# Sliding-window attention and highway FFN: one sequence of loads, half-wide stages at both ends, x transposed by DMA in the second half

## Chip, core and metric

The kernel runs on one core of a Trainium2 chip. The metric is device time in microseconds (us), the median of three runs. The engines are TensorE (PE, with its weight loads as PEld), VectorE (DVE), ScalarE (ACT), GpSimd (POOL) and SyncE (SP). POOL issues the loads that change the type from float32 to bf16, SP issues the stores; 16 DMA engines move both.

## The reference

```python
# q, k, v: (batch 8, heads 8, seq 576, head_dim 64), float32
scores = scale * np.matmul(q, k.transpose(0, 1, 3, 2))
rel = pos[:, None] - pos[None, :]
slopes = 2.0 ** (-8.0 * (np.arange(H) + 1) / H)
bias = slopes[:, None, None] * (-np.abs(rel))[None, :, :]
mask = (rel >= 0) & (rel < 128)
attn = softmax(np.where(mask, scores + bias[None], -1e9))
x = np.matmul(attn, v).transpose(0, 2, 1, 3).reshape(4608, 512)
H = np.maximum(x @ w_h, 0.0)
T = 1.0 / (1.0 + np.exp(-(x @ w_t + b_t)))
out = T * H + (1.0 - T) * x          # (4608, 512) float32
```

## The kernel before

Two batches form a duo, and there are four duos (m = 0 to 3). In a duo the rows of the tiles hold the head dimension of both batches, 64 rows each. A sequence of 576 is cut into four blocks of 128 and a tail of 64. A duo has two stages: s = 0 computes the query blocks 0 and 1 of both batches, s = 1 the blocks 2 and 3 and both tails as one block of 128 rows. A unit is one head in one stage: scores (`scores`, L274), the exponential on ACT into `pt` (`soft`, L284), the mask times decay on DVE (`mask`, L295), P.V on PE (`pv`, L310, with a column of ones that gives the sum), and the division on DVE (`norm`, L335 and L336) into `x`. That is 64 units.

q and k come in by POOL's DMAs as `ql` and `kl` (`load_qk`, L75 whole, L83 in parts of heads), their last 64 rows as `qtl` and `ktl` (`load_tails`, L95), v as `va` in five pieces (`load_v`, L104). PE transposes them (L210, L219) and DVE or ACT copies the result out (`evac`). Two sets of these tiles serve the duos in turn.

When the eight heads of a stage are normalised, its four or five blocks of 128 rows go through the FFN, 36 blocks in all: four transposes of `x` on PE (L346) and a copy on ACT (L356) give `xt`; four matmuls with wH give `pa` (L364); DVE makes max(pa, 0) - x in `uu` (L372); four matmuls with wT and one with the bias row, which contracts over a single row (L383), give `pz` (L381); ACT takes the tanh into `tt` (L390); POOL turns it into a sigmoid (L394); DVE multiplies `uu` by it (L399); POOL adds x into `ot` (L403); SP stores it (L413, L419).

The order on every engine comes from a planner at the end of the function: each piece has an engine, a cost in ns, a priority in time slots, and pieces that it needs; a list is simulated and the pieces are written out by simulated start. PSUM tiles lie in separate rings: one double bank for scores, two banks for transposes, two for P.V, one each for `pa` and `pz`. In the instruction stream each engine works strictly in its order, so a piece that waits holds all that stand behind it.

Of the kernel before, what the change touches and what calls it, by code (L numbers as in the profile page):

```python
# [10 lines left out]
P = 128  # L11
# [3 lines left out]
def kernel(  # L15
# [25 lines left out]
    SLOT, LOOK = 2200, 100  # L41
    NBLK = (4, 5)
    slopes = [float(2.0 ** (-8.0 * (h + 1) / H)) for h in range(H)]

    cp = ctx.enter_context(tc.tile_pool(name="const", bufs=1))
    p0p = ctx.enter_context(tc.tile_pool(name="p0", bufs=12))
    p1p = ctx.enter_context(tc.tile_pool(name="p1", bufs=5))
    smp = ctx.enter_context(tc.tile_pool(name="small", bufs=4))
    xp = ctx.enter_context(tc.tile_pool(name="x", bufs=3))
    fx = ctx.enter_context(tc.tile_pool(name="fx", bufs=3))  # L50
    op = ctx.enter_context(tc.tile_pool(name="ot", bufs=4))
    ft = ctx.enter_context(tc.tile_pool(name="ft", bufs=3))
    RING = {"sc": 1, "tr": 2, "av": 2, "a": 1, "z": 1}
    ps_sc, ps_tr, ps_av, ps_a, ps_z = (
        ctx.enter_context(tc.tile_pool(name="ps_" + n, bufs=b, space=PSUM))
        for n, b in RING.items()
    )
    RING.update({"p0": 12, "p1": 5, "x": 3, "xt": 3, "uu": 3, "tt": 3, "ot": 4})

# [10 lines left out]
    def load_qk(m, hs=slice(0, H), which=(0, 1)):  # L70
        i = m % 2
        for w in which:
            src, dst = ((q, QL), (k, KL))[w]
            if hs == slice(0, H):
                nc.gpsimd.dma_start(  # L75
                    out=dst[i][:].rearrange("p r h n -> p (r h) n"),
                    in_=src[2 * m : 2 * m + 2, :, 0:512, :].rearrange(
                        "r h (p t) d -> p (r h) (t d)", t=4
                    ),
                )  # L80
                continue
            for r in range(2):
                nc.gpsimd.dma_start(  # L83
                    out=dst[i][:, r, hs, :],
                    in_=src[2 * m + r, hs, 0:512, :].rearrange(
                        "h (p t) d -> p h (t d)", t=4
                    ),
                )

    def load_tails(m, which=(0, 1)):  # L90
        i = m % 2
        for w in which:
            src, dst = ((q, QTL), (k, KTL))[w]
# [16 lines left out]


# [82 lines left out]
    TR = {}  # L194
    EV = {
        (m, w, hp): "ACT" if w and (m or hp == 0) else "DVE"
        for m in range(ND) for w in (0, 1) for hp in range(5)
    }

    def transposes(m, w, hp):  # L200

        i = m % 2
        pt = ps_tr.tile([P, 1024], BF16, name="pt")
        TR[m, w, hp] = pt
        if hp < 4:
            L = (QL, KL)[w][i]
            for hl in range(2):
                for t in range(4):
                    for r in range(2):
                        nc.tensor.transpose(  # L210
                            out=pt[r * D : (r + 1) * D,
                                   hl * 512 + t * P : hl * 512 + (t + 1) * P],
                            in_=L[:, r, 2 * hp + hl, t * D : (t + 1) * D],
                            identity=ident[:],
                        )
        else:
# [8 lines left out]
    def evac(m, w, hp):  # L225
        i = m % 2
        pt = TR.pop((m, w, hp))
        cp_ = nc.scalar.copy if EV[m, w, hp] == "ACT" else nc.vector.tensor_copy
        if hp < 4:
            if w == 0:  # L230
                nc.vector.tensor_copy(
                    out=QT[i][:, 2 * hp : 2 * hp + 2, 0:512],
                    in_=pt[:].rearrange("p (h n) -> p h n", h=2),
                )
            else:
                cp_(
                    out=KT[i][:, 2 * hp : 2 * hp + 2, 0:512].rearrange(
                        "p h (c t) -> p h c t", t=4
                    ),
                    in_=pt[:].rearrange("p (h t c) -> p h c t", h=2, t=4),  # L240
                )
# [7 lines left out]
    def unit(u):
        m, r = divmod(u, 2 * H)  # L250
        s, h = divmod(r, H)
        return m, s, h

    SC, PT = {}, {}

    def scores(u):
        m, s, h = unit(u)
        i = m % 2
        sc = ps_sc.tile([P, 2, 512], F32, name="sc")
        SC[u] = sc  # L260
        qm = QT[i][:, h, 0:512].rearrange("p (t c q) -> p c t q", t=4, c=4)

        if s == 0:
            mm = ((0, 0, 2, 0), (1, 1, 2, 256))
        else:
            mm = ((2, 2, 2, 0), (3, 3, 1, 256), (3, None, 0, 384), (4, None, 0, 448))
        for j, c, n, off in mm:
# [12 lines left out]
    def soft(u):  # L280
        m, s, h = unit(u)
        pt = (p0p, p1p)[s].tile([P, 2, 512], BF16, name=f"pt{s}")
        PT[u] = pt
        nc.scalar.activation(  # L284
            out=pt[:], in_=SC.pop(u)[:], func=ACTF.Exp,
            bias=BIAS[:, h : h + 1], scale=scale,
        )

    def mask(u):
        m, s, h = unit(u)  # L290
        pt = PT[u]
        n = 2 - s
        o = pt[:].rearrange("p r (j w) -> p (r j) w", j=n)
        mk = MK[:, h : h + 1, 0 : 512 // n].to_broadcast([P, 2 * n, 512 // n])
        nc.vector.tensor_tensor(out=o, in0=o, in1=mk, op=ALU.mult)  # L295

    AV, X = {}, {}

    def pv(u):
        m, s, h = unit(u)  # L300
        i = m % 2
        va = VA[i]
        av = ps_av.tile([P, 5, D + 1], F32, name="av")
        AV[u] = av
        me = PT[u]

        def group(g, r, terms, rows=slice(0, P)):
            for n, (pt, off, j) in enumerate(terms):
                w = rows.stop - rows.start
                nc.tensor.matmul(  # L310
                    out=av[rows, g, :], lhsT=pt[:, r, off : off + w],
                    rhs=va[:, j, r, h, :],
                    start=n == 0, stop=n == len(terms) - 1,
                )

        for r in range(2):
            if s == 0:
                group(2 * r, r, ((me, 0, 0),))
                group(2 * r + 1, r, ((me, 128, 0), (me, 256, 1)))
            else:  # L320
                group(2 * r, r, ((PT[u - H], 384, 1), (me, 0, 2)))
                group(2 * r + 1, r, ((me, 128, 2), (me, 256, 3)))
        if s == 1:
            for r in range(2):
                group(4, r, ((me, 384, 3), (me, 448, 4)), slice(r * D, (r + 1) * D))
# [282 lines left out]
```

## Time and profile before

| | us |
|---|---|
| median of three runs (212.16 to 212.93) | 212.35 |
| the profiled execution, whole | 213.98 |
| its span in the trace | 212.3 |

| engine | busy us | share of the span | instructions |
|---|---|---|---|
| PE | 173.5 | 82% | 2004 |
| DVE | 142.4 | 67% | 308 |
| ACT | 124.2 | 58% | 161 |
| POOL | 119.5 | 56% | 137 |

The busy times are sums over the span. PE's is inflated where its clock is low, and matmuls are pipelined, so the time from the start of one group to the start of the next says more than the length of one. In the timeline, what stands in brackets behind a row is the time for which the engine waited before it, and what ended the wait. The SP queue issues 136 stores and nothing else.

### The profile page before, as it was taken

To read this page: it belongs to the slowest core of one execution; us is meant where nothing else is said; L and a number is where in the kernel's file an instruction comes from. 1 tells how busy PE (TensorE), PEld (TensorE's weight loads), DVE (VectorE), ACT (ScalarE), POOL (GpSimd) and SP (SyncE) were. 2 spreads that over 40 slices of the span, in tenths; PEclk is the share of its full clock that TensorE was granted. 3 is DMA by queue.
4 is the path that set the end of the run, shared out by engine and by line. 5 is a ranking of instruction groups with operands and counts; after the bars stand their busy time and mean duration, and the time that the engine had idled before them with its cause. 6 is when DMAs were issued, how large, how long until landed. Compare 5 with 4: busy or idle time off the path is not lost.

```text
span 212.3 us, 5013 instructions
## 1 busy us (share of the span) xinstructions
PE 173.5 (82%) x2004; PEld 95.4 (45%) x2004; DVE 142.4 (67%) x308; ACT 124.2 (58%) x161; POOL 119.5 (56%) x137
## 2 busy tenths in 40 slices
PE   0547765995079679999999999999999999997940
PEld 0325443573045422556565445566453455543410
DVE  5626767570094164898886988897789979873550
ACT  2340355657023544889878868877878778824420
POOL 7993493429365395845333896543345564554662
PEclk9999999999555855999999999999999999999995
DMA  5599999999999999994223999322223333324244
GB/s 60 57 195 175 181 173 141 199 172 136 121 196 212 212 165 167 127 199 124 63 54 73 109 114 186 82 54 49 57 70 77 73 79 73 79 51 99 52 98 99
DMA packets 70135, 24.97 MB, mean 118 GB/s; under 512 B 48096, under 2 KB 65504, under 8 KB 70112
## 3 DMA queue, kind: packets, MB, share of 16 engines
q0 software_dynamic: 63328, 15.21, 90.9%
q1 hardware_dynamic: 6784, 9.45, 18.1%
q8 instruction: 15, 0.25, 0.5%
q14 instruction: 8, 0.07, 0.1%
HBM read 30.41 MB, written 9.44 MB: 188 GB/s over the span
## 4 chain that ended last, share of the span: by engine, by line
PE 57%; DMA 25%; POOL 10%; issue 2%; ACT 2%; DVE 1%; POOLq 1%; SPq 0%; ACTq 0%; DVEq 0%
DMA kl<-in_k_dram 19%; PE pz L381 14%; PE pa L364 13%; PE sc L274 8%; PE av L310 8%; DMA va<-in_v_dram 6%; PE pz L383 5%; PE pt L210 4%; PE pt L346 4%; POOL va L104 3%; POOL ql L83 2%; POOL kl L83 1%; POOL ot L403 1%; ACT pt L284 1%; POOL tri L142 1%
## 5 line engine op out<-in xcount | busy, mean ns | idle before, releaser
L284 ACT ACTIVATE pt<-sc,bias 128x1024 bf16<-128x1024 f32 x64 | 71.3, 1115 | 40.9 <-PE sc L274 40.7
L403 POOL TENSOR_TENSOR ot<-uu,x 128x512 f32<-128x512 bf16 x36 | 45.4, 1262 | 21.6 <-DVE uu L399 18.1
L295 DVE TENSOR_TENSOR pt<-pt,mk 128x1024 bf16<-128x1024 bf16 x64 | 49.1, 769 | 6.0 <-ACT pt L284 5.5
L394 POOL TENSOR_SCALAR tt<-tt 128x512 f16<-128x512 f16 x36 | 23.1, 641 | 37.6 <-ACT tt L390 34.7
L310 PE MATMUL av<-va,pt 128*128 128x65 bf16 (+1 forms) x576 | 33.2, 206 | 9.5 <-DVE pt L295 8.0
L364 PE MATMUL pa<-wH,xt 128*128 128x512 bf16 x144 | 39.6, 400 | 1.2 <-ACT xt L356 0.7
L381 PE MATMUL pz<-wT,xt 128*128 128x512 bf16 x144 | 39.8, 401 | 0.2 <-ACT tt L390 0.2
L310 PEld LDWEIGHTS <-pt 128*128 128x128 bf16 (+1 forms) x576 | 25.5, 105 | 23.4 <-DVE pt L295 8.9
L390 ACT ACTIVATE tt<-pz 128x512 f16<-128x512 f32 x36 | 21.6, 599 | 22.0 <-PE pz L383 20.4
L372 DVE SCALAR_TENSOR_TENSOR uu<-pa,x 128x512 bf16<-128x512 f32 x36 | 24.7, 686 | 14.1 <-PE pa L364 14.0
L274 PE MATMUL sc<-qt,kt 64*128 64x256 bf16 (+2 forms) x384 | 28.5, 258 | 5.1 <-ACT pt L284 3.4
L336 DVE TENSOR_TENSOR x<-av,rd 128x256 bf16<-128x256 f32 (+1 forms) x64 | 29.3, 458 | 2.2
L104 POOL DMA_DIRECT2D va<-in_v_dram x20 | 22.2, 1112 | 12.7 <-DMA kl<-in_k_dram 4.2
L399 DVE TENSOR_TENSOR uu<-uu,tt 128x512 bf16<-128x512 bf16 x36 | 16.1, 448 | 17.6 <-POOL tt L394 16.8
L356 ACT COPY xt<-pt 128x512 bf16<-128x512 bf16 x36 | 20.9, 583 | 6.3 <-PE pt L346 6.2
L335 DVE RECIPROCAL rd<-av 128x4 f32<-128x4 f32 (+1 forms) x64 | 11.7, 183 | 15.6 <-PE av L310 15.1
L274 PEld LDWEIGHTS <-kt 64*128 64x128 bf16 x384 | 13.7, 98 | 16.2 <-issue 11.5
L381 PEld LDWEIGHTS <-xt 128*128 128x128 bf16 x144 | 12.3, 101 | 14.4 <-issue 4.3
L346 PE MATMUL pt<-ident,x 128*128 128x128 bf16 x144 | 15.3, 231 | 3.7 <-DVE x L336 3.7
L364 PEld LDWEIGHTS <-xt 128*128 128x128 bf16 x144 | 12.3, 100 | 12.8 <-issue 3.6
L210 PE MATMUL pt<-ident,ql 128*64 128x128 bf16 x256 | 11.8, 244 | 6.9 <-POOL ident L127 5.0
L210 PE MATMUL pt<-ident,kl 128*64 128x128 bf16 x256 | 12.9, 256 | 3.9 <-DMA kl<-in_k_dram 2.2
(42 smaller groups left out, 123.1 us busy)
## 6 DMA issues: line engine op xcount, KB each, us to landing
out_dram<-ot SPq DMA_DIRECT2D x128, 64.0 KB, 1.7
va<-in_v_dram POOLq DMA_DIRECT2D x16, 256.0 KB, 9.3
ql<-in_q_dram POOLq DMA_DIRECT2D x3, 1024.0 KB, 15.6
kl<-in_k_dram POOLq DMA_DIRECT2D x3, 1024.0 KB, 18.1
out_dram<-ot SPq DMA_DIRECT2D x8, 128.0 KB, 2.3
ql<-in_q_dram POOLq DMA_DIRECT2D x2, 384.0 KB, 5.6
kl<-in_k_dram POOLq DMA_DIRECT2D x2, 384.0 KB, 7.9
qtl<-in_q_dram POOLq DMA_DIRECT2D x8, 64.0 KB, 16.5
```

Source lines behind the costliest of these rows:

```text
L104: nc.gpsimd.dma_start(out=VA[i][0:n, c, :, :, 0:D].rearrange("s r h d -> s (r h) d"), in_=v[2 * m : 2 * m + 2, :, c * P : c * P + n, :].re ...
L210: nc.tensor.transpose(out=pt[r * D : (r + 1) * D, hl * 512 + t * P : hl * 512 + (t + 1) * P], in_=L[:, r, 2 * hp + hl, t * D : (t + 1) * D ...
L274: nc.tensor.matmul(out=sc[:, r, off : off + w], lhsT=KT[i][rows, h, j * P : (j + 1) * P], rhs=rhs, start=True, stop=True,)
L284: nc.scalar.activation(out=pt[:], in_=SC.pop(u)[:], func=ACTF.Exp, bias=BIAS[:, h : h + 1], scale=scale,)
L295: nc.vector.tensor_tensor(out=o, in0=o, in1=mk, op=ALU.mult)
L310: nc.tensor.matmul(out=av[rows, g, :], lhsT=pt[:, r, off : off + w], rhs=va[:, j, r, h, :], start=n == 0, stop=n == len(terms) - 1,)
L336: nc.vector.tensor_tensor(out=x[:, 0:nb, h * D : (h + 1) * D], in0=av[:, 0:nb, 0:D], in1=rd[:, 0:nb].to_broadcast([P, nb, D]), op=ALU.mult,)
L346: nc.tensor.transpose(out=pt[:, c * P : (c + 1) * P], in_=X[st][:, b, c * P : (c + 1) * P], identity=ident[:],)
L364: nc.tensor.matmul(out=pa[:], lhsT=xt[:, c, :], rhs=wH[:, c, :], start=c == 0, stop=c == NCK - 1)
L372: nc.vector.scalar_tensor_tensor(out=uu[:], in0=pa[:], scalar=0.0, in1=X[st][:, b, :], op0=ALU.max, op1=ALU.subtract,)
L381: nc.tensor.matmul(out=pz[:], lhsT=xt[:, c, :], rhs=wT[:, c, :], start=c == 0, stop=False)
L403: nc.gpsimd.tensor_tensor(out=ot[:], in0=UU.pop((st, b))[:], in1=X[st][:, b, :], op=ALU.add)
```

## The change

The parts of the change, in the order of the program:

- Stages are kinds now. `A` and `B` are the old two. `a`, `b`, `c`, `d` are half as wide: query block 0, 1, 2, and block 3 with the tail. Duo 0 runs as a, b, c, d, duos 1 and 2 as A, B, duo 3 as A, c, d: eleven stages. A half-wide score tile holds two heads; its exponentials are 512 instead of 1024 columns. Masks, P.V and norms work on two heads at once.
- The loads of duo 0 come in chunks of 64 partitions: rows 0 to 255 of heads 0 to 3, of heads 4 to 7, then rows 256 to 511 of all heads. The order of all loads on POOL is one written list with rising priorities, and the planner counts the time at which earlier loads land, for eight in flight.
- wH comes as float32 over SP's queue into the q tile of the second set, which is free then, and ACT casts it to bf16.
- The bias row and the row of ones are padded with zeros to 128 rows.
- From the seventh stage on (stage 6 in `DMA_X`, duo 2's A), 18 of the 36 blocks get `xt` by a DMA transpose on SP instead of four transposes on PE and a copy on ACT.
- All PSUM tiles are double banks from one ring of four; wH's and wT's products of a block share one tile.
- The planner has new costs, shifts of priority by kind of piece, and a look-ahead of its own for each engine.

```diff
+    ORDER = ("abcd", "AB", "AB", "Acd")
+    DMA_X = tuple(range(6, 20))
...
+    BUFS = {
+        "ps": 4, "pA": 6, "pB": 3, "pf": 9, "x": 3, "xt": 5, "uu": 3, "tt": 3, "ot": 3,
+    }
-    RING = {"sc": 1, "tr": 2, "av": 2, "a": 1, "z": 1}
+    def ps_tile(dt=F32):
+        return psp.tile([P, 2, 512 if dt == F32 else 1024], dt, name="ps")
...
-    ones1 = cp.tile([1, P], BF16, name="ones1")
+    ones1 = cp.tile([P, P], BF16, name="ones1")
-    bT = cp.tile([1, DM], BF16, name="bT")
+    bT = cp.tile([P, DM], BF16, name="bT")
...
+    def load_wf():
+        nc.sync.dma_start(
+            out=w_stage().rearrange("p (c n) -> p c n", c=NCK),
+            in_=moe_w_h.rearrange("(c p) n -> p c n", p=P),
+        )
+    def cast_wf():
+        nc.scalar.copy(out=wH[:].rearrange("p c n -> p (c n)"), in_=w_stage())
...
+    def soft(m, kind, h):
+        W = width(kind)
...
         nc.scalar.activation(
+            out=PT[m, kind, h // 2][:, h % 2], in_=SC[m, kind, h][:, :, o : o + W],
+            func=ACTF.Exp, bias=BIAS[:, h : h + 1], scale=scale,
+        )
...
+    def f_xd(m, kind, b):
+        xt = fx.tile([P, NCK, P], BF16, name="xt")
+        XT[m, kind, b] = xt
+        nc.sync.dma_start_transpose(out=xt[:], in_=X[m, kind][:, b, :])
...
+        if m == 0:
+            qk(0, 0)
+            qk(0, 1)
+            vv(0, 1)
+            for n_ in (1, 2):
+                seq.append((("w", n_), 850, 2650 if n_ == 1 else 10, 1, lambda n_=n_: load_w(n_), []))
+            qk(1)
+            vv(2, 3)
+            tl()
+            vv(4)
+        else:
+            qk()
+            tl()
+            vv(0, 1, 2, 3, 4)
+        for n_, (key, cost, land, n, emit, deps) in enumerate(seq):
+            node(key, "POOL", cost, pl + n_, emit, deps, land=land, n=n)
...
+                if stage_no in DMA_X:
+                    node(("x", kb), "SP", 700, t - 1.3 * dt, lambda kb=kb: f_xd(*kb), alln, take="xt", uses=[xo], land=500)
+                else:
+                    node(("xp", kb), "PE", 230, t - 1.0 * dt, lambda kb=kb: f_x(*kb), alln, take="ps", uses=[xo])
+                    node(("x", kb), "ACT", 590, t - 0.9 * dt, lambda kb=kb: f_xe(*kb), [("xp", kb)], take="xt", uses=[("xp", kb)])
...
+                    if nd[7] and e == "POOL":
+                        t = max(t, lanes[nd[8] - 1] + sync)
```

How the order moves on three queues. The first place is POOL after the loads of duo 0, in the kernel before; `ql_95`, `kl_97` and `va_103` are the second set of tiles (duos 1 and 3), `ql_94` and `kl_96` the first (duos 0 and 2).

```order
L75 DMA ql_95<-in_q_dram 128x16x256
L75 DMA kl_97<-in_k_dram 128x16x256
L95 DMA qtl_99<-in_q_dram 64x8x64 x2
L95 DMA ktl_101<-in_k_dram 64x8x64 x2
L104 DMA va_103<-in_v_dram 128x16x64 x4
L104 DMA va_103<-in_v_dram 64x16x64
L75 DMA ql_94<-in_q_dram 128x16x256
L75 DMA kl_96<-in_k_dram 128x16x256
L95 DMA qtl_98<-in_q_dram 64x8x64 x2
L95 DMA ktl_100<-in_k_dram 64x8x64 x2
L394 TENSOR_SCALAR tt<-tt 128x512
```

The same place in the changed kernel, where the second set is `ql_86`, `kl_88` and `va_94`.

```order
L101 DMA ql_86<-in_q_dram 128x16x256
L101 DMA kl_88<-in_k_dram 128x16x256
L113 DMA va_94<-in_v_dram 128x16x64
L106 DMA qtl_90<-in_q_dram 64x8x64 x2
L419 TENSOR_SCALAR tt<-tt 128x512
L106 DMA ktl_92<-in_k_dram 64x8x64 x2
L113 DMA va_94<-in_v_dram 128x16x64
L419 TENSOR_SCALAR tt<-tt 128x512
L429 TENSOR_TENSOR ot<-uu,x 128x512 x2
L113 DMA va_94<-in_v_dram 128x16x64
```

Ahead of the first `tt` stood seventeen loads of duos 1 and 2; now five of duo 1 do, and the others come between the pieces of the FFN.

The second place is POOL's beginning, in the kernel before.

```order
L83 DMA ql_94<-in_q_dram 128x2x256 x2
L83 DMA kl_96<-in_k_dram 128x2x256 x2
L126 MEMSET ident 128x128
L127 ISA
L127 AFFINE_SELECT ident<-ident 128x128
L131 IOTA kk_i 128x1
L134 MEMSET tri 128x384
L142 AFFINE_SELECT tri<-tri 128x128 x2
L142 AFFINE_SELECT tri<-tri 128x64 x2
L83 DMA ql_94<-in_q_dram 128x6x256 x2
```

And in the changed kernel, with the identity matrix first.

```order
L132 MEMSET ident 128x128
L133 ISA
L133 AFFINE_SELECT ident<-ident 128x128
L137 IOTA kk_i 128x1
L101 DMA ql_85<-in_q_dram 64x4x256 x2
L101 DMA kl_87<-in_k_dram 64x4x256 x2
L101 DMA ql_85<-in_q_dram 64x4x256 x2
L101 DMA kl_87<-in_k_dram 64x4x256 x2
L140 MEMSET tri 128x384
```

Eight pieces of q and k are issued in a row ahead of the triangles `tri`, where four were.

The third place is SP's queue, as a piece of the difference.

```order
-L419 DMA out_dram<-ot 32x512 x32
-L413 DMA out_dram<-ot 64x512 x2
-L603 UNCONDITIONAL_BRANCH
+L712 UNCONDITIONAL_BRANCH
+L197 DMA ql_86<-in_moe_w_h_dram 128x4x512
+L443 DMA out_dram<-ot 32x512 x32
+L438 DMA out_dram<-ot 64x512 x2
+L443 DMA out_dram<-ot 32x512 x20
+L372 DMA_TRANSPOSE xt<-x 128x4x128 x4
```

The queue that held stores alone now begins with wH, and DMA transposes stand between stores, the first four behind the stores of 14 blocks; five, four, two and three more follow further on.

## Rows read from the trace of the kernel before

**Rows 1.** Stretches: busy PE, PEld, DVE, ACT, POOL; clock, DMA share, GB/s
```profile
47.07:84.08 37.01, 25.32 (x229) 12.71 (x224) 14.46 (x29) 14.72 (x18) 23.28 (x25) 0.64 2.38 173
84.08:189.34 105.26, 104.86 (x1310) 57.31 (x1310) 90.06 (x198) 84.17 (x106) 56.23 (x59) 1.00 0.60 91
189.34:212.30 22.96, 13.62 (x82) 5.84 (x81) 7.93 (x14) 6.08 (x11) 11.62 (x13) 0.90 0.35 82
```

**Rows 2.** PE timeline, its last matmul: start us, length us, what, count
```profile
203.79 0.39 PE L383 MATMUL pz<-bT,ones 1*128 1x512 bf16 x1
```

**Rows 3.** PE timeline, duo 0 and duo 1; in brackets the wait before
```profile
37.94 1.89 PE L364 MATMUL pa<-wH,xt 128*128 128x512 bf16 x4
...
40.72 1.04 PE L381 MATMUL pz<-wT,xt 128*128 128x512 bf16 x4
...
59.20 0.82 PE L310 MATMUL av<-va,pt 128*128 128x65 bf16 x11 [6.65 <-DVE pt L295]
...
61.02 1.86 PE L364 MATMUL pa<-wH,xt 128*128 128x512 bf16 x4 [0.46 <-DVE uu L372]
```

**Rows 4.** DVE in order of time, its longest wait
```profile
58.12 0.42 DVE L399 TENSOR_TENSOR uu<-uu,tt 128x512 bf16<-128x512 bf16 x1 [11.36 <-POOL tt L394]
```

**Rows 5.** POOL in order of time: loads and the first FFN piece, with waits
```profile
24.49 3.18 POOL L104 DMA_DIRECT2D va<-in_v_dram  x3 [2.79 <-DMA va<-in_v_dram]
...
47.21 1.96 POOL L104 DMA_DIRECT2D va<-in_v_dram  x2 [4.16 <-DMA kl<-in_k_dram]
...
57.45 0.63 POOL L394 TENSOR_SCALAR tt<-tt 128x512 f16<-128x512 f16 x1
...
72.33 1.36 POOL L95 DMA_DIRECT2D ktl<-in_k_dram  x2 [5.96 <-DMA kl<-in_k_dram]
```

**Rows 6.** PE in order of time, two pieces of the dense stretch
```profile
93.19 0.39 PE L274 MATMUL sc<-qt,kt 64*128 64x256 bf16 x4
93.52 0.35 PE L310 MATMUL av<-va,pt 128*128 128x65 bf16 x6
93.71 0.38 PE L346 MATMUL pt<-ident,x 128*128 128x128 bf16 x4
93.93 1.03 PE L364 MATMUL pa<-wH,xt 128*128 128x512 bf16 x4
94.80 0.34 PE L310 MATMUL av<-va,pt 128*128 128x65 bf16 x6
95.07 0.40 PE L274 MATMUL sc<-qt,kt 64*128 64x256 bf16 x8
95.40 0.64 PE L210 MATMUL pt<-ident,kl 128*64 128x128 bf16 x16
95.97 1.04 PE L381 MATMUL pz<-wT,xt 128*128 128x512 bf16 x4
96.94 0.39 PE L383 MATMUL pz<-bT,ones 1*128 1x512 bf16 x1
97.26 0.40 PE L274 MATMUL sc<-qt,kt 64*128 64x256 bf16 x8
97.49 0.39 PE L219 MATMUL pt<-ident,qtl 64*128 64x64 bf16 x8
97.82 0.36 PE L310 MATMUL av<-va,pt 128*128 128x65 bf16 x6
...
99.77 0.59 PE L310 MATMUL av<-va,pt 128*128 128x65 bf16 x12
100.29 1.04 PE L381 MATMUL pz<-wT,xt 128*128 128x512 bf16 x4
```

**Rows 7.** page, part 2: GB/s moved in 40 slices of 5.3 us
```profile
GB/s 60 57 195 175 181 173 141 199 172 136 121 196 212 212 165 167 127 199 124 63 54 73 109 114 186 82 54 49 57 70 77 73 79 73 79 51 99 52 98 99
```

**Rows 8.** Page: queue 1 (packets, MB, share); 128 KB stores, us to landing
```profile
q1 hardware_dynamic: 6784, 9.45, 18.1%
...
out_dram<-ot SPq DMA_DIRECT2D x8, 128.0 KB, 2.3
```

More of the change, by code (lines that the diff above doesn't have):

```diff
@@ L191, in load_w, with chunks, tr_parts, transposes @@
             )
[L194 to L200, printed above, removed]
-        i = m % 2
[L203 to L216, printed above, removed]
+    TR, SC, PT, AV, X, XT, AZ, UU, TT, OT = ({} for _ in range(10))
+    COL = {}
+    def chunks(m):
+        return (0, 1) if ORDER[m][0] == "a" else (None,)
+    def tr_parts(m):
+        ps = [(x, hs) for x in chunks(m) for hs in range(4 if x is None else 2)]
+        return ps + ["tail"]
+    def transposes(m, w, part):
+        i = m % 2
+        if w == 0:
+            TR[m, part] = ps_tile(BF16)
+        pt = TR[m, part][:, w, :]
+        if part == "tail":
             L = (QTL, KTL)[w][i]
@@ L249, in unit @@
[L249 to L260, printed above, removed]
-        qm = QT[i][:, h, 0:512].rearrange("p (t c q) -> p c t q", t=4, c=4)
[L263 to L267, printed above, removed]
+            return
@@ new lines, in transposes @@
+        x, hs = part
+        L = (QL, KL)[w][i]
+        ps, nh = (slice(0, P), 2) if x is None else (slice(64 * x, 64 * x + 64), 4)
+        n = ps.stop - ps.start
+        for hl in range(nh):
+            for t in range(4):
+                for r in range(2):
+                    c = (hl * 4 + t) * n
+                    nc.tensor.transpose(
+                        out=pt[r * D : (r + 1) * D, c : c + n],
+                        in_=L[ps, r, nh * hs + hl, t * D : (t + 1) * D],
+                        identity=ident[ps, ps],
+                    )
@@ L284, in soft @@
         nc.scalar.activation(
-            out=pt[:], in_=SC.pop(u)[:], func=ACTF.Exp,
-            bias=BIAS[:, h : h + 1], scale=scale,
-        )
[L289 to L325, printed above, removed]
@@ L514 @@
-    SYNC, LAND, RATE = 90, 2000, 370.0
-    when, order = {}, []
-    clock = {e: 0.0 for e in ("PE", "ACT", "DVE", "POOL", "SP")}
-    rings = {n: [0.0] * RING[n] for n in ("sc", "tr", "av", "a", "z")}
-    dma = 0.0
-    todo = dict(nodes)
-    waiting = {key: len(nd[4]) for key, nd in nodes.items()}
-    users = {}
-    for key, nd in nodes.items():
-        for d in nd[4]:
-            users.setdefault(d, []).append(key)
-    ready = {e: [] for e in clock}
-    for key, nd in nodes.items():
-        if not waiting[key]:
-            ready[nd[0]].append(key)
@@ L576, with EV @@
-    order.sort(key=lambda o: o[0])
+    def EV(m, w, part):
+        return "ACT" if w and (m or part == (0, 0)) else "DVE"
+    EVC = {"DVE": (690, 1220), "ACT": (1015, 1015)}
+    UNIT = {"A": T, "B": T, "a": 0.6 * T, "b": 0.6 * T, "c": 0.6 * T, "d": 0.6 * T}
+    HALF = {"A": (330, 1118, 1340, 420, 950), "B": (370, 1118, 1340, 960, 1080),
+            "a": (210, 690, 790, 150, 640), "b": (210, 690, 790, 280, 640),
+            "c": (210, 690, 790, 280, 640), "d": (250, 690, 790, 600, 800)}
+    pos, ffn_pos, stage_no, starts = 0.0, 0.0, 0, []
@@ L577 @@
+    SHIFT = {
[4 rows of a table added]
+    }
+    LOOKS = {"PE": 206, "ACT": 0, "DVE": 9, "POOL": 35, "SP": 183}
+    order, end = plan(SHIFT, LOOKS)
     with tc.manual_schedule():
```

586 lines of the change are left out of this document (338 added, 248 removed), and 4 rows, old and new, of the table SHIFT.

## The prediction

> **What bounds the kernel now.** I read the stretches first [rows 1], since the average (PE busy 82% of the span) hides two regimes. From 84.08 to 189.34 us PE is busy 104.86 of 105.26 us at a granted clock of 1.00, while DVE (90.06), ACT (84.17) and POOL (56.23) have room: TensorE is the bound. From 47.07 to 84.08 PE is busy only 25.32 of 37.01 us, at a mean clock of 0.64. That is 25.32 x 0.64 = 16 us of full-speed work, so this stretch alone loses about 21 us. The rest of the loss lies in the start, before 47, and in the end: after PE's last matmul starts at 203.79 [rows 2] and ends at 204.2, 8.1 us pass to the end of the span at 212.3.
>
> Next, why the stretch at 47 is poor. PE waits 6.65 us for a mask of DVE and then runs slowly [rows 3]: four 512-column matmuls that last 1.04 us at 40.72 last 1.86 at 61.02. DVE had stood 11.36 us at its product with tt, which POOL had not made [rows 4]; all masks and norms queue behind it. POOL came to that tt, its first, only at 57.45 [rows 5], because in its queue all loads of duo 1 and the q, k and tails of duo 2 stand ahead of it, and loads issued there wait for earlier loads to land (2.79 us at 24.49, 4.16 us at 47.21 for kl, 5.96 us at 72.33). So loads hold POOL, POOL holds DVE, DVE holds PE, and PE's clock falls.
>
> **The yardstick.** Full-speed prices are taken from starts of one group to the next [rows 6]: a block's four wH matmuls 0.87 (93.93 to 94.80), its four wT matmuls with bias 0.97 + 0.32 = 1.29, four x transposes 0.22, a head's scores 0.33, sixteen q or k transposes 0.57, eight of a tail 0.33, 12 P.V matmuls 0.52 (0.043 each). After 84.08 PE is busy 104.86 + 13.62 = 118.5 us in before [rows 1]; 84.1 + 118.5 + 8.1 and 1.6 us of small waits at the end make the 212.3. I do the same sum for the changed kernel from another starting point: t1, when PE has passed the first k transposes of duo 1, which stand in its order behind four finished blocks and all of a, b, c of duo 0.
>
> **What remains for PE behind t1.** 32 blocks. The bias row becomes a 128-row matmul like the other four, so I price five alike: 0.87 x 5/4 = 1.09 in place of 1.29, and a block at 1.96: 62.7. Twelve sets of x transposes of duos 1 and 0 (18 of 36 blocks take their x from DMA transposes, 6 PE sets are done): 12 x 0.22 = 2.6. Transposes of q and k: 23 x 0.57 = 13.1, tails 6 x 0.33 = 2.0. Scores: 40 heads or pairs x 0.33 plus the 5 longer pairs of d at 0.4 (an estimate, 12 matmuls instead of 8) and 4 of c: 13.2 + 2 + 1.3 = 16.5. P.V: 4 d pairs (16 matmuls), 12 A (12), 8 B (24), 4 c (8), 4 d (16) = 496 x 0.043 = 21.3. Sum 118.2, say **118**. It is the same amount that before still had at 84. The change removes 18 x 0.22 = 4 us and 36 x 0.2 = 7 us in the whole kernel, and finer transposes of duo 0 (256 of 64 columns instead of 128 of 128) give some back ahead of t1. So the gain is almost wholly the distance from t1 to 84.
>
> **Where t1 lies.** Two things must come together. (a) The load of duo 1's k. In before it landed at 47.2 [rows 5]. In front of it wH leaves the POOL queue: 0.52 MB at the 181 GB/s of the third to sixth slices [rows 7] is 2.9 us less. wH instead comes as 1.05 MB of float32 on SP's queue; that queue moved 9.45 MB in 18.1% of the span [rows 8], 38.4 us, so 4.3 us more for the same 16 engines at the start. The first eight pieces are issued in one run ahead of the tri masks; the first two slices moved only 60 and 57 GB/s [rows 7], in 10.6 us what 3.5 us would do, so 0 to 7 us can be had; I take 2, since each piece is still an issue of POOL. So 46.6, from 42 to 50. (b) PE's own work ahead of it. The first v landed at 24.5 in before [rows 5]; now wT stands ahead of it too, so 24.5 + 2.9 + 4.3 - 2 = near 29. From there to t1 stand P.V of a, b, c (80 matmuls, 3.4), four blocks (7.8), six x transposes (1.3), scores (2.5), tails and one q set (1.2): 16.2 us at full speed. At the start matmuls last twice as long: 1.89 us for four at 37.94, 1.04 at 40.72 [rows 3]. All at half speed (the bound above) is 29 + 32 = 61, all at full speed 45; with half speed until 40, as in before, 29 + 11 + 10.7 = 51. Between (a) and this I take **t1 = 49**, from 44 to 58.
>
> **What is lost behind t1.** (1) Loads of duos 2 and 3 still pass through POOL between the FFN pieces: 7.1 MB at 181 GB/s is 39 us, to about 88. In the new order five DMAs of later duos stand ahead of the first tt instead of seventeen, and the others stand between the pieces, mostly one to four at a time. What is open is that a load still waits for earlier ones to land, and then holds the piece behind it. Bounds: 0, as in the dense stretch, and the 21 us of the present stretch; nearer to 0, since the block count that POOL reaches by 79 (13, walking the loads at 181 GB/s) is near what PE needs: 4 us. (2) All PSUM tiles now share one ring of four double banks: 182 tiles from about 27 to 172 us, so a tile may live 3.2 us on average; a block's (h, z, tanh: 0.87 + 1.09 + 0.6) already does 2.6. That is cover only while ACT and DVE keep up; it is in the 4 us. (3) DMA-transposed x. No row shows one. Nearest: 128 KB from SBUF over SP's queue, 2.3 us to landing [rows 8]; I take 3 us. Between the last norm of A of duo 2 and the first wH matmul on it lie about 8 us of other PE work, so it is hidden; at the very end the last three blocks wait for norm, transpose and landing behind two blocks of c (3.9 us of PE): 2 us. Far bounds: 0, and what the rival below tells. (4) The half-wide exps add one fixed cost each (24 more instructions), and the cast of wH is one ACT instruction ahead of the first k copy; ACT had 21 us to spare in 105, so nothing. The merged masks and norms only take from DVE.
>
> **Sum**: 49 + 118 + 8.1 + 4 + 2 = 181. Against the median: the span shown is 212.3 and the median 212.35, so a span is taken as the time; forecast **181 us**, its own range 170 (44 + 118 + 8, nothing lost) to 190 (t1 at 58).
>
> **Rivals.**
> *The coupling stays.* POOL's loads still come late, DVE waits at tt, the shared ring adds waits, PE idles and its granted clock drops as at 47 to 84. For it: the load rate is unchanged and POOL still issues every load in order. Against it: the first tt stands behind far fewer loads. Price: the 21 us lost there less the 4 counted: about 197 (190 to 203).
> *Transposes by DMA become the bound.* 18 of them for blocks of stages 6 to 10, one after another on SP's queue between stores. The first can start near 103 us, when A of duo 2 is normalised (t1, some 52 us of the priced work that stands ahead of it, 2 us lost); after the last some 10 us follow. The end is 103 + 18X + 10, equal to 181 at X = 3.8 us and to 212 at X = 5.5. Above 5.5 us for one the kernel is **slower than before**; X = 6 gives 221. Against it the 2.3 us row; for it that these are 2-byte elements, and that a block's x goes from TensorE's 0.22 us to a queue. Below 5.5 this rival gives 181 to 211, say 195.
> The Trainium skill (VectorE: DVE Perf Modes, The three transpose paths) gives 1309 ns for one 128x128 block by DMA and 390 by TensorE, and advises TensorE when PSUM will do. Were its four blocks per x to run in series, X would be 5.2 and the end an estimated 207; no run here shows it yet.
> *PE denser than thought*: t1 at the lowest landing, 42, PE at its high clock ahead of it, and nothing lost behind it: 42 + 118 + 8 = 168 or a little less.
>
> **How the numbers follow.** Forecast 0.63, coupling 0.17, transposes between 3.8 and 5.5 us 0.09, slower than before (X above 5.5) 0.06, denser 0.04, and 0.01 that it all cancels. Leaving out 0.06 slower, most of 0.04 below and the upper part of the two rivals, the range is 168 to 200. Faster by over 0.5% (what a measurement of this kernel can tell): 0.93; within: 0.01; slower: 0.06.
>
> **What would show it.** t1 right: the first k transposes of duo 1 on PE near 49, PE dense from there. POOL right: first tt near 36 instead of 57.45, no DVE wait at tt of over 4 us. Bias: the pz group of five in about 1.09. Transposes: landing near 3 us, no wH matmul waiting on xt before the last stage. Wrong if the granted clock is below 0.9 in 50 to 85, if PE waits for xt in duos 2 and 3, or if PE is dense but its groups are longer than priced.

## The result, and the profile after

The changed kernel takes **192.5 us** (median of four runs, 191.0 to 193.7), beside 212.6 us of the kernel before in the same comparison: a ratio of 0.905, interval 0.897 to 0.912. That is inside the range of the prediction (168 to 200), but 11.5 us above its value of 181 and 2.5 above the upper end of the range of its own case. Here and below medians and ranges are of all executions; ratios leave out those that ran clearly slower than the same kernel's fastest.

| | before | after |
|---|---|---|
| median | 212.64 | 192.53 |
| the profiled execution, whole | 213.98 | 192.25 |
| its span | 212.3 | 190.5 |
| PE busy, share | 173.5, 82% | 147.7, 78% |
| first tt on POOL | 57.45 | 34.22 |

PE in order of time, from the first P.V to t1, and POOL's first tt:

```profile
23.74 1.04 PE L347 MATMUL ps<-va,pt 128*128 128x65 bf16 x16 [1.16 <-DMA va<-in_v_dram]
...
30.88 1.68 PE L408 MATMUL ps<-wT,xt 128*128 128x512 bf16 x4
...
34.18 1.02 PE L394 MATMUL ps<-wH,xt 128*128 128x512 bf16 x4 [0.49 <-ACT tt L415]
...
48.56 0.64 PE L248 MATMUL ps<-ident,kl 128*64 128x128 bf16 x16
49.13 0.67 PE L347 MATMUL ps<-va,pt 128*128 128x65 bf16 x16
```

```profile
34.22 0.61 POOL L419 TENSOR_SCALAR tt<-tt 128x512 f16<-128x512 f16 x1 [0.37 <-ACT tt L415]
```

The first sixteen transposes of duo 1's k end at 49.1, which is t1. Four 512-column matmuls last 1.68 us at 30.88 and 1.02 from 34 on; in the kernel before they still lasted 1.86 at 61 [rows 3]. The stretches, in the columns of [rows 1]:

```profile
40.00:49.00 9.00, 7.68 (x124) 4.93 (x124) 5.88 (x14) 5.49 (x11) 6.47 (x6) 1.00 2.00 197
49.00:60.00 11.00, 9.55 (x155) 6.11 (x153) 9.27 (x17) 8.01 (x11) 9.55 (x12) 1.00 2.30 166
...
49.13:179.23 130.10, 115.20 (x1516) 67.95 (x1532) 103.48 (x171) 89.61 (x118) 82.01 (x83) 1.00 1.36 137
```

The granted clock is 1.00 where it was 0.64. From t1 to PE's last matmul 130.1 us pass. What PE waits for in them (engine, line, what ended the wait, us in total, times, longest):

```profile
PE ps L394 <- DVE x L364: 2.3, 2, 2.1
PE ps L299 <- ACT kt L273: 2.2, 4, 0.9
PE ps L394 <- ACT tt L415: 2.2, 5, 0.8
PE ps L299 <- ACT tt L415: 1.7, 3, 0.8
PE ps L394 <- DMA xt<-x: 0.9, 1, 0.9
...
PE ps L248 <- ACT tt L415: 0.8, 1, 0.8
```

With eight smaller ones these waits are 13.0 us, so at most 117.1 us are work; PE counts as busy for 115.2 of them, and the profile lacks some matmuls (it has 123 of the 144 with wH). 4.7 us of the waits end with a tanh (L415), which frees a tile of the shared ring, 2.5 with a copy of k on ACT, 1.7 with an exponential on ACT, and 3.0 lie in the last stage (2.06 for a norm, 0.92 for a DMA transpose).

The tanh is not late because ACT is busy. Ahead of each of the nine tanhs that PE waited for, ACT stood idle 0.9 to 2.0 us for DVE's `uu`. One of them, on PE, DVE and ACT:

```profile
57.09 1.02 PE L394 MATMUL ps<-wH,xt 128*128 128x512 bf16 x4
...
60.66 0.39 PE L299 MATMUL ps<-qt,kt 64*128 64x256 bf16 x4 [0.80 <-ACT tt L415]
```

```profile
59.23 0.69 DVE L400 SCALAR_TENSOR_TENSOR uu<-ps,x 128x512 bf16<-128x512 f32 x1 [0.36 <-PE ps L410]
```

```profile
60.01 0.60 ACT L415 ACTIVATE tt<-ps 128x512 f16<-128x512 f32 x1 [1.97 <-DVE uu L400]
```

`uu` needs only wH's product, but starts behind the bias matmul (L410), and the tanh starts behind `uu`: on the shared tile the steps run one after another, and the block holds its tile from 57.09 to 60.61, 3.5 us. The ends of PE, DVE, POOL and SP:

```profile
178.85 0.38 PE L410 MATMUL ps<-bT,ones 128*128 128x512 bf16 x1
```

```profile
178.00 0.41 DVE L424 TENSOR_TENSOR uu<-uu,tt 128x512 bf16<-128x512 bf16 x1
...
181.92 1.38 DVE L424 TENSOR_TENSOR uu<-uu,tt 128x512 bf16<-128x512 bf16 x1 [0.51 <-POOL tt L419]
```

```profile
183.70 1.15 POOL L429 TENSOR_TENSOR ot<-uu,x 128x512 f32<-128x512 bf16 x1 [0.68 <-DMA out_dram<-ot]
```

```profile
165.57 5.08 SPq L443 DMA_DIRECT2D out_dram<-ot  x8
170.76 3.83 SPq L372 DMA_TRANSPOSE xt<-x  x3
174.69 11.60 SPq L443 DMA_DIRECT2D out_dram<-ot  x24
186.40 1.14 SPq L438 DMA_DIRECT2D out_dram<-ot  x2
```

PE ends at 179.2, POOL at 184.85, SP issues until 187.5, and the span ends at 190.5: 11.3 us behind PE, where 8.1 were before. In the kernel before, POOL's and SP's last rows were

```profile
206.99 1.15 POOL L403 TENSOR_TENSOR ot<-uu,x 128x512 f32<-128x512 bf16 x1 [0.36 <-DVE uu L399]
```

```profile
208.47 1.11 SPq L413 DMA_DIRECT2D out_dram<-ot  x2
```

so of the 3.2 us more, 1.7 lie between PE's end and POOL's last sum (5.6 instead of 4.0), 1.2 between that and SP's last issue (2.7 instead of 1.4), and 0.3 behind it. On SP's queue the transposes hold the queue 1.21 us each and land after 2.5 us (line, engine, what, ns min/median/max; then us to landing):

```profile
L372 SPq DMA_TRANSPOSE xt<-x x18: 1188/1214/1312, 113.8 to 173.4; - x18
```

```profile
out_dram<-ot SPq DMA_DIRECT2D x128, 64.0 KB, 3.1
...
xt<-x SPq DMA_TRANSPOSE x18, 2.5
```

### The profile page after: what moved, and what is told of

Read it like the earlier page. It is cut to its first block, busy times and chain, and to the rows that moved or that the text cites. A ratio compares the mean times of both kernels' runs of the same rounds, so it can differ in the third digit from the quotient of the medians.

```text
span 190.5 us, 5091 instructions
## 1 busy us (share of the span) xinstructions
PE 147.7 (78%) x2038; PEld 89.2 (47%) x2060; DVE 138.6 (73%) x250; ACT 117.6 (62%) x168; POOL 121.7 (64%) x138
## 5 line engine op out<-in xcount | busy, mean ns | idle before, releaser
L314 ACT ACTIVATE pt<-ps,bias 128x512 bf16<-128x512 f32 (+1 forms) x88 | 72.7, 886 | 7.9 <-PE ps L299 7.9
L419 POOL TENSOR_SCALAR tt<-tt 128x512 f16<-128x512 f16 x36 | 28.1, 780 | 34.2 <-ACT tt L415 29.6
L415 ACT ACTIVATE tt<-ps 128x512 f16<-128x512 f32 x36 | 21.5, 597 | 42.8 <-DVE uu L400 40.2
L324 DVE TENSOR_TENSOR pt<-pt,mk 128x1024 bf16<-128x1024 bf16 (+1 forms) x44 | 45.2, 1033 | 2.4 <-ACT pt L314 2.4
L394 PE MATMUL ps<-wH,xt 128*128 128x512 bf16 x123 | 36.6, 385 | 9.1 <-ACT tt L415 2.7
L400 DVE SCALAR_TENSOR_TENSOR uu<-ps,x 128x512 bf16<-128x512 f32 x36 | 24.8, 690 | 25.7 <-PE ps L410 24.4
L408 PE MATMUL ps<-wT,xt 128*128 128x512 bf16 x143 | 37.6, 384 | 0.1
L299 PE MATMUL ps<-qt,kt 64*128 64x256 bf16 (+2 forms) x384 | 26.1, 249 | 6.3 <-ACT kt L273 2.4
L347 PE MATMUL ps<-va,pt 128*128 128x65 bf16 (+1 forms) x576 | 25.5, 198 | 3.9 <-DMA va<-in_v_dram 1.6
L364 DVE TENSOR_TENSOR x<-ps,rd 128x256 bf16<-128x256 f32 (+3 forms) x44 | 26.1, 594 | 1.6
L410 PE MATMUL ps<-bT,ones 128*128 128x512 bf16 x36 | 13.6, 379 | 0.0
```

The lines of the kernel that those rows point to most:

```text
L299: nc.tensor.matmul(out=sc[:, r, o + off : o + off + w_], lhsT=KT[i][rows, h, j * P : (j + 1) * P], rhs=rhs, start=True, stop=True,)
L314: nc.scalar.activation(out=PT[m, kind, h // 2][:, h % 2], in_=SC[m, kind, h][:, :, o : o + W], func=ACTF.Exp, bias=BIAS[:, h : h + 1], sca ...
L324: nc.vector.tensor_tensor(out=o, in0=o, in1=mk.to_broadcast([P, 2, rep, W]), op=ALU.mult,)
L347: nc.tensor.matmul(out=av[rows, hl, n * (D + 1) : (n + 1) * (D + 1)], lhsT=pt[:, hl, r, off : off + (D if narrow else P)], rhs=va[:, j, r, ...
L364: nc.vector.tensor_tensor(out=x.rearrange("p b (h d) -> p h b d", h=2), in0=av[:, :, :, 0:D], in1=rd[:, :, 0:nb].to_broadcast([P, 2, nb, D ...
L394: nc.tensor.matmul(out=az[:, 0, :], lhsT=XT[m, kind, b][:, c, :], rhs=wH[:, c, :], start=c == 0, stop=c == NCK - 1)
```

## Experiments

The theory: loads held POOL, POOL held DVE at its product with tt, DVE held PE and its clock; the change ends that, and from t1 on TensorE's work sets the time. All ratios are to the kernel before; the changed kernel's is 0.905.

**Loads first.** POOL's order alone is set back: eight more loads, 13 in all, stand ahead of the first tt (17 in the kernel before); the other engines keep their order.

```diff
+    pack = [key for key in keys[first:] if key[:2] in (("tl", 1), ("v", 1), ("qk", 2))]
+    keys = keys[:first] + pack + [key for key in keys[first:] if key not in pack]
```

> One part undone: on POOL all loads of duo 1 and the q and k of duo 2 stand ahead of the first tt, nearly as in the kernel before (two tails of duo 2 less); the other engines' orders are unchanged. Theory of the forecast (loads hold POOL, POOL holds DVE at the product with tt, DVE holds PE, and PE's granted clock falls): the first tt moves from 34 to about 50 us or later, DVE waits some 10 us at that product, PE idles and its clock in 40 to 70 falls below 0.9; 8 to 20 us more, 200 to 212 us. Rival (t1 came early for other reasons, the finer first stages and the order of PE, and a late tt is made up later since DVE has slack): DVE waits, but the time grows by under 4 us and the clock stays at 1.00.

207.95 us, ratio 0.981 (0.972 to 0.989): 15 us of the gain of 20 are gone. POOL, DVE and PE in order of time, and two stretches:

```profile
51.04 1.22 POOL L419 TENSOR_SCALAR tt<-tt 128x512 f16<-128x512 f16 x2
```

```profile
51.71 0.83 DVE L424 TENSOR_TENSOR uu<-uu,tt 128x512 bf16<-128x512 bf16 x1 [14.80 <-POOL tt L419]
```

```profile
53.14 0.21 PE L347 MATMUL ps<-va,pt 128*128 128x65 bf16 x1 [11.35 <-DVE x L364]
...
57.74 1.89 PE L394 MATMUL ps<-wH,xt 128*128 128x512 bf16 x4
```

```profile
40.00:49.00 9.00, 1.79 (x22) 0.99 (x21) 0.00 (x0) 0.23 (x1) 2.79 (x4) 0.76 3.30 140
49.00:60.00 11.00, 4.56 (x46) 2.61 (x46) 6.46 (x16) 3.02 (x5) 7.78 (x8) 0.50 3.02 154
```

Every link of the chain is back: the late tt, DVE's wait of 14.8 us, PE's of 11.35, then four matmuls in 1.89 us at a granted clock of 0.50, the lower level of 1.2 GHz. DVE's slack did not make it up. The place of the first FFN pieces among the loads is worth most of the change.

**Duo 0 wide.** Duo 0 runs as A, B with whole loads.

```diff
-    ORDER = ("abcd", "AB", "AB", "Acd")
-    DMA_X = tuple(range(6, 20))
+    ORDER = ("AB", "AB", "AB", "Acd")
+    DMA_X = tuple(range(4, 20))
```

> One part undone: duo 0 runs as the two wide stages A, B with whole loads of q and k (128 partitions) in place of the four half-wide ones with loads in chunks; the planner orders it anew. Transposes by DMA serve the same blocks. Theory of the forecast (the first blocks reach the FFN early because half of duo 0 is enough to begin, and so t1 lies at 49): t1 moves to 53 to 60 us, the first tt to 40 or later, and 4 to 10 us more, 197 to 203 us. Rival (t1 is set by the landing of duo 1's k, which does not depend on the stages): t1 stays within 2 us and the time within 2 us.

211.1 us (208.3 to 214.8), ratio 0.991. This run doesn't answer the question: its planner put the tails of duo 0's k behind most loads of duo 1, and PE waited 12.37 us for them at 58. So it was repeated with those tails moved ahead of duo 1's loads:

```diff
+    late = [("tl", 0, 0), ("tl", 0, 1)]
+    keys = [key for key in keys if key not in late]
+    first = keys.index(("qk", 1, 0, None, None))
+    keys = keys[:first] + late + keys[first:]
```

> Duo 0 in two wide stages as in the run before, but the tails of duo 0 are loaded ahead of the loads of duo 1; there they stood behind, and PE waited 12.4 us for ktl at 58 us. Theory of the forecast (the half-wide first stages bring the first blocks and t1 early): without that wait PE still starts later, t1 near 53 to 58 us, first tt at 40 or later, and 4 to 12 us more than the changed kernel, 197 to 205 us. Rival (the half-wide first stages are worth nothing; the run before lost its 19 us to the late tails and the slow clock behind them alone): within 3 us of the changed kernel, 190 to 196.

201.6 us, ratio 0.951 (0.944 to 0.958), 9 us more than the changed kernel, where the rival allowed 3. The rows are of an execution of 204.1 us. t1 isn't comparable, since in this order PE transposes duo 1's k early, at 44. But PE starts later and has less to do:

```profile
12.53 3.63 PE L248 MATMUL ps<-ident,ql 128*64 128x128 bf16 x64 [12.53 <-DMA ql<-in_q_dram]
...
35.31 0.63 PE L394 MATMUL ps<-wH,xt 128*128 128x512 bf16 x1
```

PE's first transposes come at 12.53 (6.76 with loads in chunks), the first wH product at 35.3 instead of 29.2, only two blocks are through before 57 where the changed kernel had four before 49, and the granted clock in 25 to 40 is 0.66 instead of 1.00. Half-wide stages and loads in chunks were undone together here, and the planner ordered everything anew, which by itself can cost as much (the shared tile, below). So the 9 us are the price of the three together; how much each is worth stays open.

**The last duo wide.**

```diff
-    ORDER = ("abcd", "AB", "AB", "Acd")
+    ORDER = ("abcd", "AB", "AB", "AB")
```

> One part undone: the last duo ends in the wide stage B instead of c and d; the planner orders it anew. Theory of the forecast (the half-wide end lets two blocks go through the FFN while the last three are still in attention): after the last norm five blocks instead of three go through PE, two more blocks at 1.96 us with nothing beside them, so 3 to 5 us more, 195 to 198 us. Rival (the end is set by SP's queue of stores and transposes, which the stages do not shorten): within 1.5 us.

196.2 us, ratio 0.918 (0.909 to 0.928), 3.6 us more, with intervals that just overlap and an order laid anew. The size fits, but it isn't only the two blocks more of PE work (rows of an execution of 197.6 us):

```profile
172.27 1.04 PE L394 MATMUL ps<-wH,xt 128*128 128x512 bf16 x4 [2.81 <-DMA xt<-x]
```

```profile
169.78 6.46 SPq L372 DMA_TRANSPOSE xt<-x  x5
176.33 15.35 SPq L443 DMA_DIRECT2D out_dram<-ot  x32
```

PE has nothing left and waits 2.81 us for the first transpose; behind five transposes 32 stores queue on SP, and the end comes 13.7 us after PE (182.2 to 195.9) instead of 11.3. SP's queue takes part.

**Transposes on PE.**

```diff
-    DMA_X = tuple(range(6, 20))
+    DMA_X = ()
```

> No DMA transposes: x goes through PE and ACT in all 36 blocks; all else as in the changed kernel, order laid out anew. Theory Q (SP's queue sets the end: 18 transposes hold SP 1.2 us each, and the last three stand ahead of 26 stores): the end behind PE's last matmul shrinks from 11.3 to 8 or 9 us, but PE gets 18 x 0.22 = 4 us and 18 more tiles in the shared ring, so 191 to 196. Rival (the transposes are pure gain, worth 4 us of PE and ACT's 10 us): 196 to 200. If they cost more than they give: under 190.

198.0 us, ratio 0.931 (0.924 to 0.939), about 5 us more, where the rival put it; 4 were priced for the DMA transposes. The order was laid anew here too, so the 5 are not shown to be theirs alone. They are no bound: 2.5 us to landing, one wait of PE of 0.9 us. They do cost at the end: without them the span ends 9.3 us behind PE (186.0 to 195.3) instead of 11.3, nearly as the theory had it (8 or 9).

**The bias as one row.**

```diff
-    ones1 = cp.tile([P, P], BF16, name="ones1")
+    ones1 = cp.tile([1, P], BF16, name="ones1")
-    bT = cp.tile([P, DM], BF16, name="bT")
+    bT = cp.tile([1, DM], BF16, name="bT")
```

> One part undone: the row of ones and the bias row are single rows again, so each block's last matmul contracts over 1 row as in the kernel before; orders of all engines are unchanged. In the trace of the changed kernel a block's wT group with the 128-row bias takes about 1.1 us of PE, in the kernel before 1.29. Theory of the forecast (a one-row matmul costs PE about 0.2 us more each, and PE is the bound behind 49 us): 32 blocks lie behind t1, so 32 x 0.2 = 6 us more, about 199 us, ratio near 0.935. Rival (PE has some 15 us of idle time behind t1, which the longer group eats, or the group is no shorter with 128 rows): 0 to 2 us more.

194.5 us, ratio 0.916 (0.910 to 0.923), about 2 more, with intervals that overlap: what the rival allowed, and not the theory's 6. PE's group in the changed kernel, and in this one:

```profile
105.69 1.03 PE L408 MATMUL ps<-wT,xt 128*128 128x512 bf16 x4
106.55 0.38 PE L410 MATMUL ps<-bT,ones 128*128 128x512 bf16 x1
106.86 0.40 PE L299 MATMUL ps<-qt,kt 64*128 64x256 bf16 x8
```

```profile
106.73 1.03 PE L406 MATMUL ps<-wT,xt 128*128 128x512 bf16 x4
107.69 0.38 PE L408 MATMUL ps<-bT,ones 1*128 1x512 bf16 x1
108.00 0.40 PE L297 MATMUL ps<-qt,kt 64*128 64x256 bf16 x8
```

From start to start the four take 0.86 ahead of the padded bias and 0.96 ahead of the one-row bias. The padded bias still takes 0.31 when scores over 64 rows follow; ahead of another 128-row matmul it takes 0.22 (102.50 to 102.72), where the one-row bias takes 0.31 (103.54 to 103.85). So the padding saves 0.1 to 0.2 us a group, not always 0.2. From t1 to PE's last piece the one-row kernel takes 3.0 us more; its t1 lies 0.7 earlier, for a reason that stays open.

**The shared tile.** The products of a block get tiles of their own, rings of one, and three double banks stay for the rest.

```diff
-        "ps": 4, "pA": 6, ...
+        "ps": 3, "pa": 1, "pz": 1, "pA": 6, ...
```

> wH's and wT's products of a block get a one-bank PSUM tile each (rings of one), and the shared ring keeps three double banks; the planner lays the order out anew. Theory S (the shared tile): in the changed kernel max(pa,0)-x starts only after wT's last matmul and tanh only after that DVE step, so a block holds a double bank for 0.87 + 1.09 + 0.8 + 0.65 = 3.4 us and PE waits some 12 us for tiles behind t1. With the tiles apart ACT's wait of 40 us on that DVE step falls under 10 us, PE waits behind t1 fall by 4 to 8 us, time 185 to 189. Rival R (the number of slots in one ring): a ring of three is shorter, PE waits stay or grow, 192 to 198.

201.8 us, ratio 0.942 (0.934 to 0.951). But the planner had ordered everything anew, so the order could be the cause. The same tiles with the changed kernel's order on every engine:

> The products with wH and wT of a block get a one-bank tile each, with rings of one; three double banks stay for the rest. Unlike in the split kernel run before, every engine keeps the order of the changed kernel. In the changed kernel the tanh waits for DVE's uu 40.2 us (29 times) and PE waits behind t1 4.7 us for slots that a tanh frees. Theory S (the shared tile makes uu and tanh run one after another, so slots come free late): the tanh no longer waits for uu, PE's waits for a tanh fall from 4.7 to about 1 us, and the time falls by 2 to 4 us, to 189 to 191. Rival R (four slots for all are worth more than an early tanh; three double banks are too few): the tanh is early but PE waits for slots of the ring of three (for norms, copies and exponentials) by 8 us or more, and the time grows by 5 to 10 us, as in the split kernel before.

192.7 us (188.8 to 195.9), too wide for a ratio. Only the execution of 188.8 us had a mean granted clock like the changed kernel's (0.978, beside 0.972 to 0.979); the other three had 0.953 to 0.967. The profiled one took 193.0:

```profile
ACT tt L418 <- PE pz L413: 32.1, 28, 5.9
```

```profile
PE pa L396 <- DVE uu L402: 4.3, 2, 3.3
```

The tanh no longer waits for uu (in the changed kernel it does for 40.2 us, 29 times), yet PE's waits from 49 on sum to 13.9 us instead of 13.0; they have other names. From t1 to PE's end 130.2 us pass instead of 130.1, so in this execution the early tanh and the fourth tile are worth about the same. Its granted clock was 0.81 in 40 to 49, where the changed kernel's was 1.00, and its t1 lies 1.7 us later. The rival R (5 to 10 us more) falls, and the split kernel had lost its 9 us by the new order. Theory S (189 to 191) is neither shown nor refuted: the one execution at the changed kernel's clock fits it, and one is too few.

**Stores on two queues.** In c and d of duo 3 two of a block's four stores go out on ACT's queue.

```diff
+                q_ = nc.scalar if late and t >= 2 else nc.sync
+                q_.dma_start(out=dst[t], in_=ot[32 * t : 32 * t + 32, :])
```

> Of the four stores of a block in duo 3's stages c and d, two are issued on ACT's queue instead of SP's; orders otherwise unchanged. Theory Q: SP issues 24 + 2 stores in 12.7 us at the end, longer than the 8.1 us that follow PE's last matmul in the kernel before, so the end shrinks from 11.3 to about 8.5 us: 189 to 190. Rival (the chain tanh, sigmoid, product, sum on ACT, POOL and DVE sets the end; POOL's last sum ends at 184.9): at most 1 us, 191.5 to 193.

192.9 us, ratio 0.897 (0.890 to 0.905), no measurable gain. The profiled span ends 10.0 us behind PE (179.9 to 189.9) instead of 11.3, so SP's issues hold about 1 us of the end. With both changes, the split tiles and the two queues:

> Both edits of e1_split and e3_stores. Theories S and Q together: the two add up, 182 to 187. If the end is set by POOL's chain, as e1_split. If R holds, no better than 190.

201.1 us, ratio 0.936 (0.926 to 0.945), like the split kernel alone.

**One store a block.**

```diff
-            for t in range(4):
-                nc.sync.dma_start(out=dst[t], in_=ot[32 * t : 32 * t + 32, :])
+            nc.sync.dma_start(out=dst, in_=ot[:])
```

> Each block of 128 rows is stored by one DMA of 256 KB in place of four of 64 KB; the order is unchanged. In the changed kernel SP issues 24 of the small stores in a row from 174.69 to 186.29 us, 0.48 us each, after three transposes that came only at 170.76 behind eight stores, and the end comes 3 us after its last issue. Theory Q (SP's queue sets the end and delays the last transposes): a 128 KB store holds SP 0.56 us, so one of 256 KB about 0.8 in place of 1.9 a block; the last transposes go out at 169.7, PE's 0.9 us wait for xt goes, SP is done within 2 us of POOL's last ot, and 2 to 4 us less, 188 to 190 us. Rival (POOL's last ot and the landing of the last store set the end, and a store of 256 KB lands later than one of 64 KB): 0 to 1 us either way.

222.4 us, ratio 1.050 (1.045 to 1.056): slower than the kernel before, 30 us above the changed one. The chain that ended last (start, us, what), and the waits for stores and transposes:

```profile
193.75 6.08 DMA xt<-x
...
207.17 6.07 DMA out_dram<-ot
```

```profile
POOL ot L429 <- DMA out_dram<-ot: 18.2, 10, 5.3
...
PE ps L394 <- DMA xt<-x: 10.6, 3, 5.4
```

The issue holds SP only 0.54 us, as hoped, but the store and the transpose that this chain shows took 6.1 us from issue to landing, where the medians of the changed kernel are 3.1 and 2.5. POOL then waits 18.2 us for buffers of ot (3.0 in the changed kernel), and with it loads and tt's are late: DVE waits 17.5 us at tt instead of 1.3, and the coupling is back. The Trainium skill (SBUF — State Buffer, The DMA setup-cost knee) advises, for transfers that are the bound, coalescing into the largest single one; here, where other work waits for each store's landing, four small ones beat one large one by far. Why a store of 256 KB lands so late is not settled.

**A lighter end.** As the stores on two queues, and for c and d of duo 3 the sigmoid's one instruction (times 0.5, plus 0.5) on DVE, with four buffers for ot, uu and tt.

```diff
-        nc.gpsimd.tensor_scalar(out=tt[:], in0=tt[:], scalar1=0.5, scalar2=0.5,
+        e_ = nc.vector if m == ND - 1 and kind in "cd" else nc.gpsimd
+        e_.tensor_scalar(out=tt[:], in0=tt[:], scalar1=0.5, scalar2=0.5,
```

> A version of the changed kernel for its end, with the order unchanged: for duo 3's c and d, two of a block's four stores (and one of the tail's two) go to ACT's queue, the sigmoid's product and sum run on DVE instead of POOL, and the buffers of ot, uu and tt are four instead of three. In the changed kernel 11.3 us pass from PE's last piece at 179.23 to the end: DVE and POOL lengthen each other (1.38 us for a product with tt that otherwise takes 0.41), POOL's last ot waits 0.68 us for a buffer and ends at 184.85, SP issues stores until 187.54, and the last lands at 190.5. Theory Q (POOL and SP's queue together hold the end): POOL's last ot ends within 4.5 us of PE's last piece instead of 5.6, the last issue comes within 1 us of it, and the end 8 us behind PE, so 2 to 4 us less, 188.5 to 190.5 us. Rival (the end is the landing of the last store, and DVE is as late with the sigmoid as POOL was): within 1 us, 191.5 to 193.5.

192.0 us, ratio 0.910 (0.902 to 0.918): the same as the changed kernel within the intervals, so the rival holds for the time. The span ends 9.6 us behind PE instead of 11.3, but a new chain of DVE and ACT takes the rest:

```profile
181.43 0.60 ACT L415 ACTIVATE tt<-ps 128x512 f16<-128x512 f32 x1 [1.77 <-DMA out_dram<-ot]
```

```profile
180.72 0.68 DVE L400 SCALAR_TENSOR_TENSOR uu<-ps,x 128x512 bf16<-128x512 f32 x1
...
182.06 1.10 DVE L420 TENSOR_SCALAR tt<-tt 128x512 f16<-128x512 f16 x1 [0.33 <-ACT tt L415]
```

The bracket at the tanh names a store, but the tanh starts at 181.43, just when DVE's uu ends at 181.40, as it does in the changed kernel. DVE's uu stands behind the sigmoid step of the block before, and that step lasts 1.10 us beside POOL's sum, 0.28 without.

## Why the prediction was right, and where its sizes were off

By its own sum: 49 + 118 + 8.1 + 4 + 2 = 181.1.

- *t1 = 49*: measured 49.1, near in part by luck. The mechanism is shown: the first tt, expected near 36, came at 34.2, DVE waits at tt 1.3 us in all, and the loads-first run takes the early t1 away again. The two paths that were to meet at t1 were both off. Duo 1's k, issued at 28.10, landed 16.1 us later, at 44.2 (46.6 expected), and PE came to it only at 48. PE's own path began at 23.7, with the first v, and not near 29. The row that gave 24.5 for the kernel before shows the second piece of v; the first had landed already when POOL went on here:

```profile
21.15 0.55 POOL L186 DMA_DIRECT2D bT<-in_moe_b_t_dram  x1 [1.50 <-DMA va<-in_v_dram]
```

From the first v to t1 PE then took 25.4 us, with 4.3 us of waits that the sum did not have, instead of some 22 (51 less 29). An earlier start and a longer way balanced.
- *118 us of PE work*: measured 117.1 at most. The bias, priced at 0.2 us a block, gave 0.1 to 0.2.
- *4 + 2 us of waits behind t1*: measured 13.0. **This is the step that was mis-sized.** The 4 were meant for loads coupling through POOL, with the shared ring "in the 4 us". The coupling went to almost nothing, but PE waited 4.7 us for tanhs, 2.5 for k's copies, 1.7 for exponentials and 3.0 in the last stage, where 2 were priced. The prediction counted a block's hold on its tile as wH, wT and tanh, 2.6 us, within the 3.2 that a ring of four allows on average. It left out uu, which on the shared tile stands between wT and the tanh; in the row shown the hold is 3.5. "ACT had 21 us to spare in 105, so nothing" did not help, as ACT was idle, waiting for DVE, ahead of those tanhs. That the shared tile costs time in the end is not shown: with tiles apart PE waits as long for other things, in the one execution that was profiled. Which of these waits another order could avoid stays open.
- *8.1 us at the end*: measured 11.3. It was carried over from the kernel before, though the change puts three transposes (3.8 us of SP) between the last stores and lets 24 of them queue behind. SP's new work was counted for landing only, not for issue. That is a part of the cause: without transposes the end is 9.3, with stores on two queues 10.0. The larger part, 1.7 us, lies between PE's end and POOL's last sum, where DVE and POOL lengthen each other and POOL waits 0.7 us for a buffer that a store held.
- *A span is taken as the time*: the profiled run of before is 213.98 for a span of 212.3, and after 192.25 for 190.5, so 1.7 more each time. That the span of before met the median was chance. The table ahead of the prediction had both numbers.

Together, from 181.1: +0.1 - 0.9 + 7.0 + 3.2 give the span of 190.5, and 2.0 more the median of 192.5.

Two rivals came nearer in time with the wrong mechanism. *Transposes by DMA become the bound* (say 195) falls: 1.21 us of queue and 2.5 us to landing where 3.8 were allowed. *The coupling stays* (197) falls too: the loads-first run is that case, and it takes 208. The estimate of 5.2 us from the Trainium skill's 1309 ns for one block (VectorE: DVE Perf Modes, The three transpose paths) took the four blocks of an x in series; the trace doesn't bear that out.

The prices of the parts, each undone alone, are 15, 9, 5, 4 and 2 us. They sum to more than the gain of 20, so they overlap, and three of them (9, 5, 4) include a new order.

## What to carry to other kernels

When a queue both issues loads and computes, ask which compute pieces stand behind which loads: moving eight loads behind the first pieces was worth more here than any work that was taken away. Price a shared buffer by how long one user holds it, with every step on the way; another engine's share of busy time does not tell whether its result comes in time. A planner that lays the order anew is a change of its own: keep the order when one part is tested. An end with more transfers on a queue needs its own sum of issues, and one transfer in place of four needs a run before it is believed.

## What the runs showed of the hardware

- The last 256 KB store on the chain, of 128 partitions, took 6.1 us from issue to landing, with an issue of 0.54 us; 64 KB stores took 3.1 us in the changed kernel and 1.7 in the kernel before (medians), and a transpose among the large stores 6.1 instead of 2.5.
- DVE's product of 0.41 us lasts 1.38 beside POOL's sum, and its 0.28 us step 1.10. The Trainium skill (Trainium Architecture — The Big Picture, What this means for kernel authors) says that DVE and GpSimd contend for one pair of ports; the rows agree.
- A change in the number of rows that matmuls contract over cost about 0.1 us in the groups compared here: four 128-row matmuls took 0.96 us ahead of a one-row one and 0.86 ahead of a 128-row one; the bias took 0.31 ahead of a matmul of another row count (one row ahead of 128, 128 ahead of 64) and 0.22 between two of 128.
